# Weight decoding around the last attention group: bits moved from VectorE to ScalarE, a shorter PReLU, another order

## The chip, the cores and the metric

The kernel runs on one core of one Trainium2 chip. The metric is device time in microseconds. Three runs of the kernel before took 809.04, 806.07 and 810.14 us, a median of 809.04. Engines are named TensorE (PE: matmuls and transposes), ScalarE (ACT), VectorE (DVE), GpSimd (POOL) and SyncE (SP, which here issues nearly all loads).

## The reference

Three stages on 2304 tokens (4 batches of 576) of 512 features. Heads 0 to 3 attend to the last 32 positions, heads 4 to 7 to every 32nd:

```python
scores = np.where(masks, scale * q @ k.T, -1e9)      # 8 heads of 64
x = softmax(scores) @ v                              # -> (2304, 512)
h = x @ w_in                                         # 512 -> 2048
g = np.maximum(h, 0.0) + alpha * np.minimum(h, 0.0)  # PReLU, alpha per column
x = g @ w_out                                        # 2048 -> 512
logits = x @ w_gate; e = argmax(logits)              # 8 experts
y = np.maximum(x[e] @ w1[e], 0.0) @ w2[e]            # 512 -> 1024 -> 512
out = softmax(logits)[e] * sigmoid(x @ w_output_gate)[e] * y
```

`w_in` and `w_out` arrive as 64-bit floats, and the kernel turns them into 32-bit ones itself.

## The kernel before, in words

**Tiling.** The MLP's hidden dimension is cut into 16 parts of 128 (`NC1`), the tokens into 6 blocks of 384. One part of the weights is a tile of 128 x 1024 64-bit numbers, `w_in` and `w_out` side by side. Step n = 16 * block + part computes `mlp_in(n)` (12 matmuls of 384 columns into the bank `h`), PReLU (`mlp_act`), a split into high and low halves (`mlp_split`: `gh` by ScalarE, `gl` by VectorE) and `mlp_out(n)` (9 matmuls of 512 columns into three `acc` banks that gather over a block). Every product is computed in three matmuls, high by high, low by high, high by low, so that activations (`xh`, `xl`) and weights (`w`, 2048 wide, both halves) exist as pairs. `h` has two buffers: `mlp_in(n+2)` waits until `gl` of step n has read its bank.

**Decoding.** A part c goes through five operations before it can be used, each 128 x 1024: `decode_a` (ScalarE, L402, rescales the upper 32-bit word so that the exponent fits), `decode_b` (VectorE: L406 shifts left by three, L407 ORs in the top three bits of the lower word), `decode_s` (VectorE, L413, sets the sign), `decode_c` (ScalarE, L420, casts to the high half), `decode_d` (VectorE, L424, the low half). All 16 parts are decoded once, during the prologue and block 0.

**Order.** Every engine's instructions stand in the order in which the code is written; nothing is reordered. The prologue is a loop over 13 attention steps: step s computes the scores of group s, the exponentials and the norm of s - 1, the transposes of s - 2, the values of s - 3 with their store (ScalarE: `xh`) and rest (VectorE: `xl`, L372). Groups 0 to 9 cover what block 0 of the MLP needs; the last of them is group 9, whose rest is in step 12. Between these, decoding of part k starts in step 2 + 2k (`T0`) and advances by one operation per step, so parts 0 to 4 are begun there, and the first quarters of `mlp_in(0)` and `mlp_in(1)` are spread over steps 10 to 12 (`PRE`). Behind the prologue stand the last quarters of these two, their PReLU and split, 7 filler matmuls (`WAKE`), and the rest of the decoding of part 3. Then the loop over n: its iteration n issues `mlp_in(n+2)`, `mlp_act(n+2)`, parts of the decoding of n + 4, n + 5 and n + 6, `mlp_out(n)`, `mlp_split(n+2)`, and in the first 14 iterations of a block the pieces of one attention group for the next blocks. The bank `T` is shared by the transposes and the values of these groups: the transposes wait until the `xl` of the values before has been taken out.

**Loads** go out on SyncE in program order: `qk`, `v`, weight parts (`load_ws`). The router's weights are split once into `wg_hl`, in step 4 of the prologue.

Of the kernel before, what the change touches and what calls it, by code (L numbers as in the profile page):

```python
# [15 lines left out]
P = 128  # L16
# [8 lines left out]
E = 8  # L25
# [29 lines left out]

WHEN = ((0, 7), (1, 1), (1, 1), (1, 4), (1, 6))

NRV = range(FIRST)
FS = {2: 2}

PRE = {10: ((0, range(2)),), 11: ((0, range(2, 3)), (1, range(2))), 12: ((1, range(2, 3)),)}
QL = 96
RS = 7
NEG = -1.0e9
BIG = 12582912.0
SIGN = -(2**31)

C_ID = 0
C_I8 = C_ID + P
# [14 lines left out]
def attention_prelu_mlp_routed_experts_kernel(  # L84
# [19 lines left out]

    cst = base.tile([P, C_END], F32, name="cst")
    alpha_sb = base.tile([P, NC1], F32, name="alpha_sb")
    nalpha = base.tile([P, NC1], F32, name="nalpha")
    wg_sb = base.tile([P, KD, 2 * E], F32, name="wg_sb")
    cst16 = base.tile([P, W_END], BF16, name="cst16")
    wg_hl = base.tile([P, KD, 4 * E], F32R, name="wg_hl")  # L110
# [14 lines left out]
    with tc.manual_schedule():  # L125
# [47 lines left out]
        def load_v(n):  # L173
            b, pr, gs = visits[n]
            c = slice(2 * gs[0], 2 * gs[-1] + 2) if pr < 2 else slice(0, 5)
            t = v_t[n] = apool.tile([P, 6, 2, D], F32, tag="v", name="v", bufs=3)
            src = qkv[b, pr, :, 2 * S :].rearrange("p (i h d) -> p i h d", i=6, h=2)
            nc.sync.dma_start(t[:, c], src[:, c])
# [217 lines left out]
        def words(c):  # L396
            two = raw_t[c].rearrange("p (n two) -> p n two", two=2)
            return two[:, :, 0], two[:, :, 1]

        def decode_a(c):  # L400
            t = dec_t[c] = stage()[:, :1024]
            nc.scalar.activation(out=t, in_=words(c)[1].bitcast(F32), func=AF.Copy, scale=2.0**-112)  # L402

        def decode_b(c):
            t = dec_t[c].bitcast(I32)
            nc.vector.tensor_scalar(out=t, in0=t, scalar1=3, scalar2=None, op0=ALU.logical_shift_left)  # L406
            nc.vector.scalar_tensor_tensor(  # L407
                out=t, in0=words(c)[0], scalar=29, in1=t, op0=ALU.logical_shift_right, op1=ALU.bitwise_or
            )

        def decode_s(c):
            t = dec_t[c].bitcast(I32)
            nc.vector.scalar_tensor_tensor(  # L413
                out=t, in0=words(c)[1], scalar=SIGN, in1=t, op0=ALU.bitwise_and, op1=ALU.bitwise_or
            )
            raw_t.pop(c)

# [29 lines left out]
        def mlp_act(n):  # L447
            c = n % NC1
            ph = h_t.pop(n)
            v = ph[:, :BLK]  # L450
            a = xpool.tile([P, BLK], F32, tag="a", name="a", bufs=2)
            nc.scalar.activation(out=a, in_=v, func=AF.Relu)  # L452
            nc.scalar.activation(out=v, in_=v, func=AF.Relu, scale=-1.0)  # L453
            nc.vector.scalar_tensor_tensor(  # L454
                out=v, in0=v, scalar=nalpha[:, c : c + 1], in1=a, op0=ALU.mult, op1=ALU.add
            )
            h_t[n] = v

# [614 lines left out]

        load_qk(0)
        nc.vector.memset(zeros, 0.0)
        nc.scalar.activation(out=nalpha[:, 0:1], in_=zeros[:, 0:1], func=AF.Exp)
        warm(bank("acc0"), WARM)
        loads = iter(range(NC1))

# [11 lines left out]
        nc.sync.dma_start(alpha_sb, alpha)  # L1091
        nc.sync.dma_start(wg_sb, wg)
        load_qk(2)
        load_qk(3)
        load_v(2)
        load_ws(1)

        span = [0, FIRST + EXTRA]
        on = lambda g: span[0] <= g < span[1]
# [28 lines left out]

        steps_of = [(0, FIRST + LV), (FIRST + EXTRA, 23), (23, 31), (31, 39), (39, NG + LV)]
        NPRO = steps_of[0][1]  # L1130
        T0 = [2 + 2 * k for k in range(DEC + 1)]
        steps_done = {}

        def decode(k, n):
# [6 lines left out]
        for s in range(NPRO):  # L1141
            att_step(s, ("h", "h") if s % 2 else ("S", "X"), "acc0" if s % 2 else "T", "acc1" if s % 2 else "acc2")
            for n, ks in PRE.get(s, ()):
                mlp_in(n, ks)
            if s % 2 == 0:
                load_ws(1)
            if s == 4:
                nc.vector.tensor_scalar_mul(nalpha, alpha_sb, -1.0)
                nc.scalar.activation(out=wg_hl[:, :, : 2 * E], in_=wg_sb, func=AF.Copy)
                nc.vector.tensor_tensor(  # L1150
                    out=wg_hl[:, :, 2 * E :], in0=wg_sb, in1=wg_hl[:, :, : 2 * E].bitcast(F32), op=ALU.subtract
                )
                nc.vector.memset(acc_oh[:, 0, :], 0.0)
            for k in range(len(T0)):
                if 0 <= s - T0[k] and s < NPRO - 1:
                    decode(k, s - T0[k] + 1)

        span[:] = [FIRST + EXTRA if EXTRA < LV else 0, NG]
        for n in range(2):
            mlp_in(n, range(KD - 1, KD))  # L1160
            mlp_act(n)
            mlp_split(n)
        warm(bank("acc0"), WAKE)
        decode(DEC - 1, 5)
        decode(DEC, 3)
        decode(DEC + 1, 1)
        last = NBLK * NC1
        turn_at, logits_at = {}, {}
        for blk in range(NBLK - 1):
# [13 lines left out]
        for n in range(last):  # L1183
# [324 lines left out]
```

## Time and profile before

| | |
|---|---|
| median of three runs | 809.04 us (806.07 to 810.14) |
| profiled execution | 808.35 us, span 806.6 us |
| TensorE busy | 779.9 us, 97% of the span |
| VectorE busy | 469.7 us, 58% |
| ScalarE busy | 427.8 us, 53% |
| GpSimd busy | 90.9 us, 11% |
| mean granted clock of TensorE | 0.99 of full speed |

Busy shares are means over the whole span. The prologue lies in the first 45 us, block 0 of the MLP ends near 146 us, the blocks of the MLP end near 540 us, and the experts take the rest. A wait that the profile shows on an engine is idle time just before an instruction, with what ended it.

### The profile page before, as it was taken

What the parts mean: (1) busy time and instruction counts of PE and PEld (TensorE: products, weight loads), DVE (VectorE), ACT (ScalarE), POOL (GpSimd) and SP (SyncE); (2) the same over time, 40 slices, a digit from 0 to 9 for tenths busy, and PEclk for the clock granted to TensorE, in tenths of its full rate; (3) what the DMA queues carried; (4) which work ended last, traced back from release to release, by engine and by line L of the source; (5) the groups of instructions that cost most, each with busy time, mean ns of one, the idle gap of its engine ahead of it and who ended that gap; (6) DMA issues with size and microseconds to landing.
All of it is one profiled execution on the core that took longest, in us unless ns stands there. A gap on an engine that the chain in (4) does not pass through costs nothing.

```text
span 806.6 us, 13674 instructions
## 1 busy us (share of the span) xinstructions
PE 779.9 (97%) x5050; PEld 655.1 (81%) x5050; DVE 469.7 (58%) x1041; ACT 427.8 (53%) x1057; POOL 90.9 (11%) x91
## 2 busy tenths in 40 slices
PE   8798999999999999999999999999999999999996
PEld 4476777888888888888898888889889877978884
DVE  5989995346434553556233434668696557855432
ACT  6867785454544454645343333265544558665442
POOL 0001111011101011111000000100202121213201
PEclk9999999999999999999999999999999999999998
DMA  9818212012100131101000100543225578867510
GB/s 333 327 40 358 100 38 81 1 34 86 64 2 18 31 108 47 47 1 40 1 1 1 40 1 1 224 181 118 67 71 191 187 280 297 304 237 260 198 66 32
DMA packets 22620, 91.04 MB, mean 113 GB/s; under 512 B 3082, under 2 KB 7312, under 8 KB 15376
## 3 DMA queue, kind: packets, MB, share of 16 engines
q1 hardware_dynamic: 18816, 78.52, 26.5%
q0 software_dynamic: 3728, 11.55, 4.1%
q8 instruction: 42, 0.69, 0.3%
q14 instruction: 34, 0.28, 0.1%
HBM read 105.78 MB, written 9.97 MB: 144 GB/s over the span
## 4 chain that ended last, share of the span: by engine, by line
PE 77%; DVE 12%; issue 4%; ACT 3%; DMA 3%; SPq 0%; another core or an unknown queue 0%; POOL 0%; ACTq 0%; POOLq 0%; DVEq 0%
PE acc L1054 10%; PE acc L477 8%; PE h L444 7%; PE h L443 7%; PE h L445 7%; PE acc L479 7%; PE acc L478 7%; PE T L328 2%; PE sl_bank L234 2%; DMA raw<-in_wp_dram 2%; DVE stage L407 2%; PE T L313 2%; PE h L977 1%; DVE w L424 1%; PE h L978 1%
## 5 line engine op out<-in xcount | busy, mean ns | idle before, releaser
L900 DVE TENSOR_TENSOR wx<-raw,wx 128x1024 fp32r<-128x1024 f32 x96 | 112.1, 1220 | 41.5 <-ACT wx L899 38.2
L443 PE MATMUL h<-xh,w 128*128 128x384 f32 x384 | 129.7, 338 | 1.1 <-DVE gl L464 0.8
L444 PE MATMUL h<-xl,w 128*128 128x384 f32 x384 | 129.2, 337 | 0.7 <-DVE xl L372 0.7
L445 PE MATMUL h<-xh,w 128*128 128x384 f32 x384 | 129.0, 336 | 0.0
L454 DVE SCALAR_TENSOR_TENSOR h<-h,nalpha,a 128x384 f32<-128x384 f32 x96 | 59.9, 624 | 113.9 <-ACT h L453 113.9
L477 PE MATMUL acc<-w,gh 128*128 128x512 f32 x288 | 125.0, 434 | 0.0
L479 PE MATMUL acc<-w,gl 128*128 128x512 f32 x288 | 114.3, 397 | 0.0
L478 PE MATMUL acc<-w,gh 128*128 128x512 f32 x288 | 114.0, 396 | 0.0
L452 ACT ACTIVATE a<-h 128x384 f32<-128x384 f32 x96 | 47.2, 491 | 102.5 <-PE h L445 102.4
L899 ACT ACTIVATE wx<-raw 128x1024 fp32r<-128x1024 f32 x96 | 94.8, 1056 | 6.4 <-DMA raw<-in_wexp_dram 6.4
L1054 PE MATMUL acc<-wx,hh 128*128 128x512 f32 x304 | 96.9, 400 | 0.0
L443 PEld LDWEIGHTS h<-xh,w 128*128 128x128 f32 x384 | 72.3, 188 | 6.5 <-DVE gl L464 1.8
L444 PEld LDWEIGHTS h<-xl,w 128*128 128x128 f32 x384 | 72.2, 188 | 4.9 <-DVE xl L372 1.0
L297 POOL TENSOR_TENSOR p<-p,sm 96x512 f32<-96x512 f32 (+2 forms) x38 | 35.6, 936 | 345.3 <-DVE sm L296 239.6
L445 PEld LDWEIGHTS h<-xh,w 128*128 128x128 f32 x384 | 72.2, 188 | 0.0
L464 DVE TENSOR_TENSOR gl<-h,gh 128x384 fp32r<-128x384 f32 x96 | 53.3, 555 | 31.9 <-PE acc L479 17.2
L1054 PEld LDWEIGHTS acc<-wx,hh 128*128 128x128 f32 x304 | 56.4, 190 | 11.2
L479 PEld LDWEIGHTS acc<-w,gl 128*128 128x128 f32 x288 | 54.5, 189 | 13.2
L463 ACT ACTIVATE gh<-h 128x384 fp32r<-128x384 f32 x96 | 46.7, 486 | 34.3 <-DVE h L454 34.1
L477 PEld LDWEIGHTS acc<-w,gh 128*128 128x128 f32 x288 | 54.3, 189 | 10.6 <-issue 0.3
L1054 PE MATMUL acc<-wx,hl 128*128 128x512 f32 x152 | 60.1, 395 | 0.0
L478 PEld LDWEIGHTS acc<-w,gh 128*128 128x128 f32 x288 | 54.8, 190 | 5.5
(257 smaller groups left out, 1399.5 us busy)
## 6 DMA issues: line engine op xcount, KB each, us to landing
raw<-in_wexp_dram SPq DMA_DIRECT2D x64, 1024.0 KB
raw<-in_wp_dram SPq DMA_DIRECT2D x16, 1024.0 KB
qk<-in_qkv_dram SPq DMA_DIRECT2D x10, 576.0 KB
rows<-stage SPq DMA_DIRECT2D x15, 256.5 KB
v<-in_qkv_dram SPq DMA_DIRECT2D x8, 320.0 KB
qk<-in_qkv_dram SPq DMA_DIRECT2D x4, 384.0 KB
v<-in_qkv_dram SPq DMA_DIRECT2D x6, 256.0 KB
qk<-in_qkv_dram SPq DMA_DIRECT2D x4, 224.0 KB
```

Source lines behind the costliest of these rows:

```text
L443: mm(ph[:, :BLK], w_in(c, 0, k), xh[:, k, :], start=(k == 0), stop=False)
L444: mm(ph[:, :BLK], w_in(c, 0, k), xl[:, k, :], start=False, stop=False)
L445: mm(ph[:, :BLK], w_in(c, 1, k), xh[:, k, :], start=False, stop=(k == KD - 1))
L452: nc.scalar.activation(out=a, in_=v, func=AF.Relu)
L454: nc.vector.scalar_tensor_tensor(out=v, in0=v, scalar=nalpha[:, c : c + 1], in1=a, op0=ALU.mult, op1=ALU.add)
L464: nc.vector.tensor_tensor(out=gl, in0=v, in1=gh.bitcast(F32), op=ALU.subtract)
L477: mm(o, gh[:, t], w_out(c, 0), start=(c == 0), stop=False)
L478: mm(o, gh[:, t], w_out(c, 1), start=False, stop=False)
L479: mm(o, gl[:, t], w_out(c, 0), start=False, stop=(c == NC1 - 1))
L899: nc.scalar.activation(out=w[:, :1024], in_=raw, func=AF.Copy)
L900: nc.vector.tensor_tensor(out=w[:, 1024:], in0=raw, in1=w[:, :1024].bitcast(F32), op=ALU.subtract)
L1054: mm(po[i], h[:, h0 : h0 + P], wk[:, w0 : w0 + 512], start=st, stop=sp)
```

## The change

- *Six parts, three bits.* For the even parts from 4 on (`TAIL`: 4, 6, 8, 10, 12, 14) ScalarE writes the top three bits of the lower word into the low 16 bits of the upper word, in the raw tile, right behind `decode_a`; it reads and writes 16-bit integers that lie eight bytes apart. VectorE leaves out the OR of L407 there, and `decode_s` takes sign and tail in one mask (`SIGN + 7`).
- *PReLU.* ScalarE computes relu(-h) once into the SBUF tile `a`, and VectorE h + (1 - alpha) * a. The second ScalarE operation goes; `nalpha` becomes `calpha`.
- *Order.* A table (`DEC_AT`) says in which prologue step which part is taken how far. Part 2 is finished in step 12 behind the last group's rest; part 3 gets only shift and OR in the prologue, its sign, cast and low half stand behind the first PReLU; part 4 is begun behind them and finished in iteration 0 of the loop, ahead of part 5. The first three quarters of `mlp_in(1)` are split differently over step 12 and behind.
- *Loads.* The second weight part is loaded ahead of `v` 2 and `qk` 3.
- *Router.* `wg_hl` and a small memset move from prologue step 4 to iteration 13.

```diff
+TAIL = range(4, NC1, 2)
-PRE = {10: ((0, range(2)),), 11: ((0, range(2, 3)), (1, range(2))), 12: ((1, range(2, 3)),)}
+PRE = {10: ((0, range(2)),), 11: ((0, range(2, 3)),), 12: ((1, range(2)),)}
+DEC_AT = {
+    2: ((0, 1),),
+    3: ((0, 2),),
+    4: ((0, 3), (1, 1)),
+    5: ((0, 4), (1, 2)),
+    6: ((0, 5), (1, 3), (2, 1)),
+    7: ((1, 4), (2, 2)),
+    8: ((1, 5), (2, 3), (3, 1)),
+    10: ((2, 4), (3, 2)),
+    12: ((2, 5),),
+}
+SIGN_AND_TAIL = SIGN + 7
@@ decode_a
             nc.scalar.activation(out=t, in_=words(c)[1].bitcast(F32), func=AF.Copy, scale=2.0**-112)
+            if c in TAIL:
+                q = raw_t[c].bitcast(U16).rearrange("p (n four) -> p n four", four=4)
+                nc.scalar.activation(
+                    out=q[:, :, 2], in_=q[:, :, 1], func=AF.Copy, scale=2.0**-13, bias=2.0**-14 - 0.5
+                )
@@ decode_b
             nc.vector.tensor_scalar(out=t, in0=t, scalar1=3, scalar2=None, op0=ALU.logical_shift_left)
-            nc.vector.scalar_tensor_tensor(
-                out=t, in0=words(c)[0], scalar=29, in1=t, op0=ALU.logical_shift_right, op1=ALU.bitwise_or
-            )
+            if c not in TAIL:
+                nc.vector.scalar_tensor_tensor(
+                    out=t, in0=words(c)[0], scalar=29, in1=t, op0=ALU.logical_shift_right, op1=ALU.bitwise_or
+                )
@@ decode_s
-                out=t, in0=words(c)[1], scalar=SIGN, in1=t, op0=ALU.bitwise_and, op1=ALU.bitwise_or
+                scalar=SIGN_AND_TAIL if c in TAIL else SIGN,
...
@@ mlp_act
-            nc.scalar.activation(out=a, in_=v, func=AF.Relu)
-            nc.scalar.activation(out=v, in_=v, func=AF.Relu, scale=-1.0)
+            nc.scalar.activation(out=a, in_=v, func=AF.Relu, scale=-1.0)
             nc.vector.scalar_tensor_tensor(
-                out=v, in0=v, scalar=nalpha[:, c : c + 1], in1=a, op0=ALU.mult, op1=ALU.add
+                out=v, in0=a, scalar=calpha[:, c : c + 1], in1=v, op0=ALU.mult, op1=ALU.add
             )
@@ loads
         load_qk(2)
+        load_ws(1)
+        load_v(2)
         load_qk(3)
-        load_v(2)
-        load_ws(1)
@@ prologue loop
             if s == 4:
-                nc.vector.tensor_scalar_mul(nalpha, alpha_sb, -1.0)
-                nc.scalar.activation(out=wg_hl[:, :, : 2 * E], in_=wg_sb, func=AF.Copy)
...
+                nc.vector.tensor_scalar(
+                    out=calpha, in0=alpha_sb, scalar1=-1.0, scalar2=1.0, op0=ALU.mult, op1=ALU.add
+                )
-            for k in range(len(T0)):
-                if 0 <= s - T0[k] and s < NPRO - 1:
-                    decode(k, s - T0[k] + 1)
+            for k, n in DEC_AT.get(s, ()):
+                decode(k, n)
@@ behind the prologue
-        for n in range(2):
-            mlp_in(n, range(KD - 1, KD))
-            mlp_act(n)
-            mlp_split(n)
+        mlp_in(0, range(KD - 1, KD))
+        mlp_in(1, range(2, KD))
         warm(bank("acc0"), WAKE)
+        mlp_act(0)
+        mlp_split(0)
+        mlp_act(1)
+        decode(DEC - 1, 3)
+        mlp_split(1)
         decode(DEC - 1, 5)
-        decode(DEC, 3)
-        decode(DEC + 1, 1)
+        decode(DEC, 1)
@@ loop over n
+            if n == 0:
+                decode(DEC, 5)
             if n + DEC + 1 < NC1:
                 decode(n + DEC + 1, 3)
...
+            if n == NC1 - 3:
+                nc.scalar.activation(out=wg_hl[:, :, : 2 * E], in_=wg_sb, func=AF.Copy)
...
```

In the rows of order that follow, `raw_192`, `raw_279`, `raw_367` and `raw_364` are the raw tiles of parts 3, 4 and 5 (5 has another number after), `raw_454` and `raw_451` that of part 6, `acc_506`/`acc_499`, `acc_543`/`acc_536` and `acc_574`/`acc_556` the values of groups 7, 8 and 9; a stage tile without a raw one beside it is the part being shifted or subtracted. VectorE at the end of the prologue, before, from the rest of group 7 to the first PReLU:

```order
L372 TENSOR_TENSOR xl<-acc_506,xh 128x2x12x7
L372 TENSOR_TENSOR xl<-acc_506,xh 128x2x6x7
L424 TENSOR_TENSOR w<-stage,w 128x1024
L413 SCALAR_TENSOR_TENSOR stage<-raw_192,stage 128x1024
L372 TENSOR_TENSOR xl<-acc_543,xh 128x2x12x7
L372 TENSOR_TENSOR xl<-acc_543,xh 128x2x6x7
L406 TENSOR_SCALAR stage<-stage 128x1024
L407 SCALAR_TENSOR_TENSOR stage<-raw_279,stage 128x1024
L372 TENSOR_TENSOR xl<-acc_574,xh 128x12x4
L372 TENSOR_TENSOR xl<-acc_574,xh 128x6x4
L454 SCALAR_TENSOR_TENSOR h<-h,nalpha,a 128x384
```

The same place of VectorE after the change:

```order
L388 TENSOR_TENSOR xl<-acc_499,xh 128x2x12x7
L388 TENSOR_TENSOR xl<-acc_499,xh 128x2x6x7
L427 TENSOR_SCALAR stage<-stage 128x1024
L429 SCALAR_TENSOR_TENSOR stage<-raw_192,stage 128x1024
L388 TENSOR_TENSOR xl<-acc_536,xh 128x2x12x7
L388 TENSOR_TENSOR xl<-acc_536,xh 128x2x6x7
L388 TENSOR_TENSOR xl<-acc_556,xh 128x12x4
L388 TENSOR_TENSOR xl<-acc_556,xh 128x6x4
L451 TENSOR_TENSOR w<-stage,w 128x1024
L481 SCALAR_TENSOR_TENSOR h<-a,calpha,h 128x384
L491 TENSOR_TENSOR gl<-h,gh 128x384
```

Part 3's shift and OR (which stood ahead of group 9's norm) now stand behind group 7's rest; part 2's low half moved behind group 9's rest, and part 3's sign and part 4's shift and OR have left this place. VectorE from the second split of the start to the split of iteration 0, before:

```order
L464 TENSOR_TENSOR gl<-h,gh 128x384
L424 TENSOR_TENSOR w<-stage,w 128x1024
L413 SCALAR_TENSOR_TENSOR stage<-raw_279,stage 128x1024
L454 SCALAR_TENSOR_TENSOR h<-h,nalpha,a 128x384
L406 TENSOR_SCALAR stage<-stage 128x1024
L407 SCALAR_TENSOR_TENSOR stage<-raw_367,stage 128x1024
L413 SCALAR_TENSOR_TENSOR stage<-raw_367,stage 128x1024
L424 TENSOR_TENSOR w<-stage,w 128x1024
L464 TENSOR_TENSOR gl<-h,gh 128x384
```

VectorE at the same place after the change:

```order
L491 TENSOR_TENSOR gl<-h,gh 128x384
L451 TENSOR_TENSOR w<-stage,w 128x1024
L481 SCALAR_TENSOR_TENSOR h<-a,calpha,h 128x384
L427 TENSOR_SCALAR stage<-stage 128x1024
L435 SCALAR_TENSOR_TENSOR stage<-raw_279,stage 128x1024
L451 TENSOR_TENSOR w<-stage,w 128x1024
L427 TENSOR_SCALAR stage<-stage 128x1024
L429 SCALAR_TENSOR_TENSOR stage<-raw_364,stage 128x1024
L435 SCALAR_TENSOR_TENSOR stage<-raw_364,stage 128x1024
L491 TENSOR_TENSOR gl<-h,gh 128x384
```

Part 3's sign now stands just ahead of these rows, between the second PReLU and its split; part 4's shift, sign and low half stand ahead of part 5 and so of the `gl` of iteration 0, and no OR is there for part 4. ScalarE from the first PReLU of the start to the split of iteration 0, before:

```order
L452 ACTIVATE a<-h 128x384
L453 ACTIVATE h<-h 128x384
L463 ACTIVATE gh<-h 128x384
L452 ACTIVATE a<-h 128x384
L453 ACTIVATE h<-h 128x384
L463 ACTIVATE gh<-h 128x384
L402 ACTIVATE stage<-raw_367 128x1024
L452 ACTIVATE a<-h 128x384
L453 ACTIVATE h<-h 128x384
L420 ACTIVATE w<-stage 128x1024
L402 ACTIVATE stage<-raw_454 128x1024
L463 ACTIVATE gh<-h 128x384
```

ScalarE at the same place after the change:

```order
L490 ACTIVATE gh<-h 128x384
L480 ACTIVATE a<-h 128x384
L490 ACTIVATE gh<-h 128x384
L447 ACTIVATE w<-stage 128x1024
L418 ACTIVATE stage<-raw_279 128x1024
L421 ACTIVATE raw_279<-raw_279 128x1024
L480 ACTIVATE a<-h 128x384
L447 ACTIVATE w<-stage 128x1024
L418 ACTIVATE stage<-raw_364 128x1024
L418 ACTIVATE stage<-raw_451 128x1024
L421 ACTIVATE raw_451<-raw_451 128x1024
L490 ACTIVATE gh<-h 128x384
```

One activation per PReLU is gone. Between the second `gh` and the PReLU of iteration 0 stand the cast of part 3 (L447), `decode_a` of part 4 (L418) and the new pass (L421, raw to raw); parts 5 and 6 follow behind the cast of part 4, with the pass of part 6 ahead of the last `gh`.

## Rows read from the trace of the kernel before

**Rows 1.** First part of the page: busy us, share of the span, instructions per engine.
```profile
PE 779.9 (97%) x5050; PEld 655.1 (81%) x5050; DVE 469.7 (58%) x1041; ACT 427.8 (53%) x1057; POOL 90.9 (11%) x91
```

**Rows 2.** Stretches: from:to us, length, busy us per engine, clock, DMA share, GB/s.
```profile
20.00:40.00 20.00, 15.38 (x113) 9.21 (x114) 19.07 (x47) 17.98 (x67) 0.00 (x0) 0.91 0.84 334
...
60.00:80.00 20.00, 16.78 (x97) 13.14 (x96) 19.66 (x33) 15.86 (x45) 3.09 (x3) 0.94 0.90 359
...
80.00:130.00 50.00, 48.62 (x323) 38.58 (x323) 45.67 (x88) 38.02 (x119) 7.05 (x8) 0.99 0.24 80
...
100.00:120.00 20.00, 19.44 (x130) 15.56 (x129) 19.69 (x36) 17.00 (x55) 2.48 (x3) 1.00 0.13 39
...
140.00:540.00 400.00, 398.89 (x2395) 342.91 (x2393) 189.90 (x536) 182.26 (x541) 28.41 (x30) 1.00 0.13 47
```

**Rows 3.** TensorE's waits, 45 to 140 us: waiter, releaser, us in total, times, longest.
```profile
PE T L313 <- DVE xl L372: 3.6, 4, 2.2
```

**Rows 4.** Timeline of TensorE: start, duration, line, operands, shapes, idle before and releaser.
```profile
37.66 0.65 PE L313 MATMUL T<-cst,p 126*126 126x126 f32 x4 [1.55 <-DVE p L297]
...
44.19 0.44 PE L443 MATMUL h<-xh,w 128*128 128x384 f32 x1 [0.25 <-ACT xh L367]
...
45.37 0.44 PE L444 MATMUL h<-xl,w 128*128 128x384 f32 x1 [0.74 <-DVE xl L372]
...
58.27 0.37 PE L443 MATMUL h<-xh,w 128*128 128x384 f32 x1
...
77.06 0.69 PE L313 MATMUL T<-cst,p 126*126 126x126 f32 x4 [2.21 <-DVE xl L372]
...
79.26 0.63 PE L478 MATMUL acc<-w,gh 128*128 128x512 f32 x1
...
86.83 0.34 PE L443 MATMUL h<-xh,w 128*128 128x384 f32 x1
...
131.25 0.39 PE L479 MATMUL acc<-w,gl 128*128 128x512 f32 x1
...
131.48 0.34 PE L443 MATMUL h<-xh,w 128*128 128x384 f32 x1
...
137.66 0.34 PE L443 MATMUL h<-xh,w 128*128 128x384 f32 x1
```

**Rows 5.** Timeline of VectorE, 63 to 77 us: two `gl` in a row.
```profile
63.49 0.55 DVE L464 TENSOR_TENSOR gl<-h,gh 128x384 fp32r<-128x384 f32 x1
...
69.66 0.55 DVE L464 TENSOR_TENSOR gl<-h,gh 128x384 fp32r<-128x384 f32 x1
```

**Rows 6.** Timeline of VectorE, 18 to 46 us, the prologue.
```profile
18.99 0.21 DVE L1150 TENSOR_TENSOR wg_hl<-wg_sb,wg_hl 128x64 fp32r<-128x64 f32 x1
...
21.42 0.17 DVE L295 TENSOR_SCALAR sm<-sm 126x4 f32<-126x4 f32 x1 [0.41 <-ACT p L281]
...
40.59 1.21 DVE L424 TENSOR_TENSOR w<-stage,w 128x1024 fp32r<-128x1024 f32 x1
...
41.73 1.21 DVE L413 SCALAR_TENSOR_TENSOR stage<-raw,stage 128x1024 int32<-128x1024 int32 x1
...
43.97 1.23 DVE L407 SCALAR_TENSOR_TENSOR stage<-raw,stage 128x1024 int32<-128x1024 int32 x1
...
45.11 0.29 DVE L372 TENSOR_TENSOR xl<-acc,xh 128x48 fp32r<-128x48 f32 x2
```

**Rows 7.** Timeline of ScalarE, 18 to 47 us.
```profile
18.61 1.16 ACT L402 ACTIVATE stage<-raw 128x1024 f32<-128x1024 f32 x1 [1.50 <-DMA raw<-in_wp_dram]
...
46.02 0.49 ACT L452 ACTIVATE a<-h 128x384 f32<-128x384 f32 x1 [1.81 <-PE h L445]
...
46.41 0.49 ACT L453 ACTIVATE h<-h 128x384 f32<-128x384 f32 x1
```

**Rows 8.** All instructions of one line: count, duration min/median/max in ns, first and last start.
```profile
L402 ACT ACTIVATE stage<-raw x16: 1122/1148/1167, 11.1 to 111.7; 128x1024 f32<-128x1024 f32 x16
...
L407 DVE SCALAR_TENSOR_TENSOR stage<-raw,stage x16: 1224/1226/1226, 15.8 to 118.8; 128x1024 int32<-128x1024 int32 x16
```

More of the change, by code (lines that the diff above doesn't have):

```diff
@@ L9 @@
 F32R = mybir.dt.float32r
+U16 = mybir.dt.uint16
 BF16 = mybir.dt.bfloat16
@@ L106, in attention_prelu_mlp_routed_experts_kernel @@
     alpha_sb = base.tile([P, NC1], F32, name="alpha_sb")
-    nalpha = base.tile([P, NC1], F32, name="nalpha")
+    calpha = base.tile([P, NC1], F32, name="calpha")
     wg_sb = base.tile([P, KD, 2 * E], F32, name="wg_sb")
@@ L413, in decode_s @@
             nc.vector.scalar_tensor_tensor(
-                out=t, in0=words(c)[1], scalar=SIGN, in1=t, op0=ALU.bitwise_and, op1=ALU.bitwise_or
+                out=t,
+                in0=words(c)[1],
+                scalar=SIGN_AND_TAIL if c in TAIL else SIGN,
+                in1=t,
+                op0=ALU.bitwise_and,
+                op1=ALU.bitwise_or,
             )
@@ L1075, in attention_prelu_mlp_routed_experts_kernel @@
         nc.vector.memset(zeros, 0.0)
-        nc.scalar.activation(out=nalpha[:, 0:1], in_=zeros[:, 0:1], func=AF.Exp)
+        nc.scalar.activation(out=calpha[:, 0:1], in_=zeros[:, 0:1], func=AF.Exp)
         warm(bank("acc0"), WARM)
@@ L1130, in attention_prelu_mlp_routed_experts_kernel @@
         NPRO = steps_of[0][1]
-        T0 = [2 + 2 * k for k in range(DEC + 1)]
         steps_done = {}
@@ L1147, in attention_prelu_mlp_routed_experts_kernel @@
             if s == 4:
-                nc.vector.tensor_scalar_mul(nalpha, alpha_sb, -1.0)
-                nc.scalar.activation(out=wg_hl[:, :, : 2 * E], in_=wg_sb, func=AF.Copy)
-                nc.vector.tensor_tensor(
-                    out=wg_hl[:, :, 2 * E :], in0=wg_sb, in1=wg_hl[:, :, : 2 * E].bitcast(F32), op=ALU.subtract
-                )
-                nc.vector.memset(acc_oh[:, 0, :], 0.0)
-            for k in range(len(T0)):
-                if 0 <= s - T0[k] and s < NPRO - 1:
-                    decode(k, s - T0[k] + 1)
+                nc.vector.tensor_scalar(
+                    out=calpha, in0=alpha_sb, scalar1=-1.0, scalar2=1.0, op0=ALU.mult, op1=ALU.add
+                )
+            for k, n in DEC_AT.get(s, ()):
+                decode(k, n)
         span[:] = [FIRST + EXTRA if EXTRA < LV else 0, NG]
-        for n in range(2):
-            mlp_in(n, range(KD - 1, KD))
-            mlp_act(n)
-            mlp_split(n)
+        mlp_in(0, range(KD - 1, KD))
+        mlp_in(1, range(2, KD))
         warm(bank("acc0"), WAKE)
+        mlp_act(0)
[3 more added lines that the diff above has]
+        mlp_split(1)
         decode(DEC - 1, 5)
-        decode(DEC, 3)
-        decode(DEC + 1, 1)
+        decode(DEC, 1)
         last = NBLK * NC1
@@ L1235, in attention_prelu_mlp_routed_experts_kernel @@
                 mlp_split(n + 2)
+            if n == NC1 - 3:
+                nc.scalar.activation(out=wg_hl[:, :, : 2 * E], in_=wg_sb, func=AF.Copy)
+                nc.vector.tensor_tensor(
+                    out=wg_hl[:, :, 2 * E :], in0=wg_sb, in1=wg_hl[:, :, : 2 * E].bitcast(F32), op=ALU.subtract
+                )
+                nc.vector.memset(acc_oh[:, 0, :], 0.0)
             if c == NC1 - 1 and blk == 3:
```

## The prediction

> **What bounds the kernel now.** I began with the page's first part: TensorE is busy for 779.9 of 806.6 us [rows 1]. So nearly everything hangs on TensorE, and a change elsewhere can win only where TensorE waits or runs slowly. The stretches tell where that is [rows 2]. From 140 to 540 us it is idle for 1.1 us of 400 while VectorE is under half busy: nothing off TensorE moves the time there. From 20 to 40 us it is idle for 4.6 us, from 60 to 80 us for 3.2 us at a mean clock of 0.94, from 80 to 130 us for 1.4 us. In 20 to 40 and 60 to 80 us VectorE is busy for 19.07 and 19.66 of 20 us, from 100 to 120 us for 19.69. It decodes the weights there, and this is what the change touches.
>
> TensorE's waits between 45 and 140 us name the releaser [rows 3]: VectorE's `xl`, attention's remainder, 3.6 us. In order of time: at 77.06 TensorE waits 2.21 us for the T bank, which this `xl` frees, and the matmuls behind it show 0.63 us where one of their kind shows 0.39 at 131.25: the lower of the two clock levels, 1.2 GHz [rows 4]. Where TensorE alone decides, a step with attention takes 137.66 - 131.48 = 6.18 us; from 86.83 to 131.48 seven steps take 6.38 each, 1.4 us over in all [rows 4]. VectorE's step is as long: `gl` follows `gl` by 69.66 - 63.49 = 6.17 us [rows 5]. Two engines with the same period: relief of VectorE is worth something only until TensorE's 6.18 is reached.
>
> The last wait before the loop is the other place: TensorE sits until 45.37 for the last group's `xl` [rows 4], which VectorE does at 45.11 behind decoding of parts 2, 3 and 4 [rows 6].
>
> **The change part by part.** *End of the prologue.* Ahead of the last `xl` VectorE runs L424 (1.21), L413 (1.21) and a shift with L407 (1.23) between 40 and 45.11 us [rows 6]; part 3's shift and OR stand before these. Afterwards only part 3's shift and OR remain ahead of it, where VectorE waits for TensorE and ScalarE anyway. What is late next is TensorE's own queue: before, it ran from the transposes at 37.66 to the first missing `xh` (0.25 us before 44.19) without a wait, 6.28 us [rows 4]; the three matmuls that end this stretch now stand behind the first product's last three, so the length stays. Its start comes 0.65 us sooner: the subtraction of `wg_hl` (0.21) leaves VectorE's queue, and VectorE's wait of 0.41 us at 21.42 goes [rows 6], because ScalarE no longer waits 1.50 us at 18.61 for the second weight part [rows 7], whose load goes out ahead of one `qk` and one `v` load. These two land later, at worst when that part landed before, near 18.6, and attention step 7 needs them first, three steps on: cost nothing; with that cover gone it would be the 1.5 us back. So the first PReLU activation starts at 37.0 + 6.3 = 43.3 instead of 46.02 [rows 7]: 2.7 us earlier.
>
> *Filling the loop.* That work was moved, not removed. Behind the first activation VectorE now has part 3's sign and subtraction and part 4's shift, sign and subtraction, all before part 5's and before `gl` of step 2, for which TensorE's third product (58.27 before [rows 4]) waits. ScalarE stands in it too: the cast of part 3, L402 of part 4 and its new pass come before the activation of step 2, so VectorE waits about 1.4 us there, and 1.0 us for the cast of part 4. With the durations of rows 6 and 8: activation of step 2 at 43.3 + 7.0 = 50.3; VectorE's PReLU at 50.8, shift and sign to 53.2, subtraction 54.2 to 55.3, part 5 to 58.3, `gl` to 58.8. The third product starts at 58.9, 0.6 us later than before. TensorE (fillers to 46.1, then two products and two outputs of 2.1 each, 12 matmuls 0.174 and 9 matmuls 0.234 us apart, and scores of 1.0) is through at 55.5 and idle for 3.4 us; it may lose its clock, which is hidden, since its next scores wait for exponentials till about 62.6. The 2.7 us are spent.
>
> *One OR less in six parts.* L407 costs 1.226 us [rows 8]; parts 4, 6, 8, 10, 12 and 14 lose it, 7.4 us of VectorE. Part 4's is in the sum above; from step 1 on every second step of VectorE is 1.2 us shorter than 6.17, the mean about 5.6, under TensorE's 6.18. Carried on with the same durations, `gl` of step 3 starts at 62.9, 0.6 us earlier than at 63.49, and two steps on another 1.2; the wait of 2.21 us at 77.06 goes, and with it the slow stretch (six matmuls of 512 columns at 0.2 us more, two of 384 at 0.15: 1.5). So of 2.2 + 1.5 = 3.7 the 0.5 that is still owed goes off: the product at 86.83 [rows 4] starts at 83.6, 3.2 us gained. From there TensorE can gain its remaining 1.4 us.
>
> *The new ScalarE pass.* No row shows 2-byte elements eight bytes apart. The nearest is L402, which reads the same tile at the same step: 1.148 us [rows 8], and I take that. Below, it could halve with the bytes (0.57); above, double if two-byte writes run apart (2.3). ScalarE's own bound on the step: 17.00 us in 20 us [rows 2] is 5.45 per step of 6.41, less 0.39 for the PReLU activation (start to start, 46.02 to 46.41 [rows 7]), 5.06; with the pass 6.2, about TensorE's 6.18. So in a tail step ScalarE has no room, and the exponentials behind it come late; I charge 0.1 us for four such steps, 0.4. The Trainium skill speaks against the move: "ScalarE: Activation LUTs", section "Rules for kernel authors", gives additions and multiplications to VectorE, as up to about three times as fast per element there in bf16. The trace disagrees for this pair, 1.226 against 1.148 [rows 8].
>
> *PReLU.* L453 goes (0.49 us, 96 times [rows 7]); VectorE's operation keeps one operand in PSUM, and I take its time as unchanged (between 0.55, the row of `gl` [rows 5], and 0.7). Off block 0 the shorter chain is slack: it is worth between 0 and TensorE's 1.1 idle us of 140 to 540 [rows 2], and I take 0. The `wg_hl` pair moves to step 13 of block 0, where the decoding is over and its reader is a block away: nothing.
>
> Sum: 3.2 + 1.4 - 0.4 = 4.2. The profiled execution took 808.35 us (span 806.6), so 804.15 in its terms; it lies 0.7 under the median of the runs, 809.04, so I forecast 804.8.
>
> **Rivals.** *Nothing is spent on filling.* If the third product starts 2.7 us earlier too, the gain is that plus the idle 3.2 and 1.4 us of 60 to 130 [rows 2] plus 1.5 of slow clock, 8.8: 800.2. For it: less ScalarE work per step, and the pass may be short. Against it: VectorE's order, with 5 us of decoding ahead of that product.
>
> *The fill costs more.* If the 3.4 us of idle TensorE bring the low clock and the slow product pushes scores and exponentials, the loop starts some 2 us further behind, and the relief of the ORs meets TensorE's 6.18 before it is made good: 3.2 - 2.0 = 1.2 is left: 807.8. For it: the stall at 77.06 was followed by slow matmuls [rows 4]. Against it: the slack before the exponentials.
>
> *ScalarE takes VectorE's place (slower).* At 2.3 us per pass, ScalarE's tail step is 5.06 + 2.3 = 7.4, 1.2 over TensorE's 6.18. Six such steps cost 7.1, since ScalarE works in order and has the exponentials and the cast of the next weight part behind the pass: 804.8 + 7.1 = 811.9. It decides from 1.12 us per pass on, and eats the whole gain at 1.8. For it: such an access is in no row. Against it: L402 on the same bytes. By the skill's factor of three on 1.226 the pass would be an estimated 3.7 us and the time about 820.
>
> **How the numbers follow.** Forecast 0.58 (its own range 801.5 to 807.5), no fill cost 0.17, costlier fill 0.15, ScalarE 0.10. What a measurement of this kernel can tell from no change is 0.5%, 4 us, so the line is at 805.0. The forecast lies just on the fast side: 0.34 of its 0.58 there; with 0.17 faster is 0.51. Same: 0.24 + 0.15 + 0.03 of the ScalarE case, 0.42. Slower: 0.07. The range 800.0 to 809.5 leaves out half of the second case and most of the ScalarE one.
>
> **What would show it.** In the new profile: the first PReLU activation near 43.3; the third product of the loop near 58.9 with some 3 us of idle TensorE ahead; no wait of TensorE for `xl` over 1 us; VectorE with gaps of about 1 us in every second step between 75 and 120; the product that started at 86.83 near 83.6, the one at 137.66 near 133.5; the new pass at 1.1 to 1.2 us; from 140 us on the same spacing as before. Wrong it is if the pass takes 1.8 us or more, if the third product starts before 57 or after 60.5, or if TensorE waits for ScalarE's exponentials more than 1 us in all between 85 and 130.

## The result, and the profile after

The changed kernel takes 817.21 us (median of 5 runs, 815.63 to 818.81) against 809.04 for the kernel before on the same chip, a ratio of 1.0103 [1.008 to 1.0127]: 8.2 us slower. I had forecast 804.8 and faster. Its profiled execution took 818.81 us (span 816.6).

The first part of the page of the changed kernel gives each engine's busy us, share of the span and instructions:

```profile
PE 785.2 (96%) x5050; PEld 661.0 (81%) x5050; DVE 463.4 (57%) x1035; ACT 405.2 (50%) x967; POOL 91.8 (11%) x91
```

Beside [rows 1]: TensorE has as many matmuls and is busy 5.3 us longer, so part of the loss is matmuls at the lower clock; the other part is waiting. The stretches of the changed kernel (start:end, length, busy us and instructions of PE, PEld, DVE, ACT, POOL, then granted clock, DMA share and GB/s) say where:

```profile
40.00:60.00 20.00, 15.32 (x86) 12.09 (x84) 12.98 (x19) 12.82 (x17) 0.00 (x0) 1.00 0.27 89
60.00:80.00 20.00, 17.85 (x96) 15.04 (x97) 17.77 (x32) 18.00 (x46) 3.09 (x3) 0.83 0.47 193
80.00:130.00 50.00, 45.41 (x291) 36.64 (x290) 41.91 (x82) 41.45 (x106) 5.59 (x7) 0.97 0.31 109
140.00:540.00 400.00, 399.19 (x2409) 343.07 (x2404) 187.62 (x536) 151.26 (x462) 29.00 (x31) 1.00 0.13 43
```

From 80 to 130 us TensorE is idle for 4.6 us, where [rows 2] have 1.4; from 60 to 80 us its mean clock is 0.83 against 0.94. From 140 to 540 us the stretch is again full. VectorE, busy for 19.66 of 20 us from 60 to 80 us before, has room now (17.77), and ScalarE rose there from 15.86 to 18.00, from 80 to 130 us from 38.02 to 41.45. TensorE's waits of the changed kernel, up to 150 us (who waits <- for whom: us in all, times, longest):

```profile
PE h L470 <- DVE gl L491: 6.0, 1, 6.0
PE sl_bank L244 <- ACT p L297: 3.7, 4, 1.5
PE sl_bank L244 <- DVE gl L491: 1.2, 1, 1.2
```

The `xl` that led [rows 3] is gone. In its place stand one wait of 6.0 us for `gl` and several for ScalarE's exponentials (`p`, L297). The same waits in order of time, with the first product of the loop's next block at the end (start, us, engine, line, operation, out<-in, [idle before <-releaser]; TensorE of the changed kernel):

```profile
61.35 0.69 PE L470 MATMUL h<-xh,w 128*128 128x384 f32 x1 [6.03 <-DVE gl L491]
61.83 0.52 PE L471 MATMUL h<-xl,w 128*128 128x384 f32 x1
...
86.10 0.27 PE L244 MATMUL sl_bank<-cst 96*96 96x256 bf16 x1 [1.47 <-ACT p L297]
...
90.37 0.63 PE L504 MATMUL acc<-w,gh 128*128 128x512 f32 x1
...
101.61 0.27 PE L244 MATMUL sl_bank<-cst 126*126 126x252 bf16 x1 [1.48 <-ACT p L297]
...
115.45 0.27 PE L244 MATMUL sl_bank<-cst 96*96 96x256 bf16 x1 [1.16 <-DVE gl L491]
...
143.70 0.34 PE L470 MATMUL h<-xh,w 128*128 128x384 f32 x1
```

The third product starts at 61.35 instead of 58.27 [rows 4], after a stall, and its matmuls take 0.52 us where 0.34 is the normal one: 1.2 GHz, until 67.3 (granted clock 0.51 from 61.0 to 67.3). Behind the wait at 86.10 the 512-column matmuls take 0.63 where 0.39 is normal, the same lower clock; behind the waits at 101.61 and 115.45 they do not. The product that stood at 137.66 [rows 4] stands at 143.70, so 6.0 us are lost by the end of block 0. The last PReLU of the loop begins at 541.8 (before 536.3), so 5.5 of them are left there.

What ScalarE does ahead of that `gl` (same columns, ScalarE of the changed kernel):

```profile
43.30 0.49 ACT L480 ACTIVATE a<-h 128x384 f32<-128x384 f32 x1 [1.46 <-PE h L472]
...
48.21 1.12 ACT L418 ACTIVATE stage<-raw 128x1024 f32<-128x1024 f32 x1
49.37 2.52 ACT L421 ACTIVATE raw<-raw 128x1024 uint16<-128x1024 uint16 x1
51.63 0.58 ACT L480 ACTIVATE a<-h 128x384 f32<-128x384 f32 x1
54.75 1.06 ACT L447 ACTIVATE w<-stage 128x1024 fp32r<-128x1024 f32 x1 [2.54 <-DVE stage L435]
55.72 2.14 ACT L418 ACTIVATE stage<-raw 128x1024 f32<-128x1024 f32 x2
57.89 2.50 ACT L421 ACTIVATE raw<-raw 128x1024 uint16<-128x1024 uint16 x1
60.13 0.57 ACT L490 ACTIVATE gh<-h 128x384 fp32r<-128x384 f32 x1
```

The first activation is at 43.30, as forecast. The new pass, L421, takes 2.5 us, not 1.148. It runs twice, for part 4 and part 6, ahead of `gh` at 60.13, which `gl` needs. All six, in the view of that line (min/median/max ns):

```profile
L421 ACT ACTIVATE raw<-raw x6: 2497/2570/2612, 49.4 to 111.9; 128x1024 uint16<-128x1024 uint16 x6
```

VectorE's PReLU is what I took it for (L481, median 0.621 us; before, L454, 0.626).

My theory from here: **the price of the pass makes the loss**. Rivals: **the order** (the last group's chain ahead of the decoding leaves a hole in front of the third product, whatever the pass costs), and **the PReLU form**.

### The profile page after: what moved, and what is told of

It reads as the page before. It is cut to its first block, busy times and chain, and to the rows that moved or that the text cites. A ratio compares the mean times of both kernels' runs of the same rounds, so it can differ in the third digit from the quotient of the medians.

```text
span 816.6 us, 13575 instructions
## 1 busy us (share of the span) xinstructions
PE 785.2 (96%) x5050; PEld 661.0 (81%) x5050; DVE 463.4 (57%) x1035; ACT 405.2 (50%) x967; POOL 91.8 (11%) x91
## 4 chain that ended last, share of the span: by engine, by line
PE 81%; DVE 9%; ACT 5%; issue 3%; DMA 2%; POOL 0%; ACTq 0%; POOLq 0%; DVEq 0%
PE acc L1081 10%; PE acc L504 9%; PE h L470 8%; PE h L472 8%; PE h L471 8%; PE acc L506 7%; PE acc L505 7%; PE sl_bank L250 3%; PE T L344 2%; PE T L329 2%; PE h L1004 2%; ACT raw L421 2%; PE h L1005 2%; PE h L1006 2%; DVE wx L927 1%
## 5 line engine op out<-in xcount | busy, mean ns | idle before, releaser
L481 DVE SCALAR_TENSOR_TENSOR h<-a,calpha,h 128x384 f32<-128x384 f32 x96 | 59.5, 620 | 87.1 <-ACT a L480 84.2
```

The source lines that it names most:

```text
L481: nc.vector.scalar_tensor_tensor(out=v, in0=a, scalar=calpha[:, c : c + 1], in1=v, op0=ALU.mult, op1=ALU.add)
```

## The experiments

All ratios below are against the kernel before, run on the same chip as the experiment.

**The pass taken out.** The changed kernel with VectorE's OR in all parts:

```
-TAIL = range(4, NC1, 2)
+TAIL = ()
```

> The changed kernel without the new ScalarE pass (all 16 parts get their OR on VectorE again); order, loads and PReLU stay changed. Pass theory: the pass, 2.57 us in the trace of after, is what made it slower; without it the activation of step 2 comes about 2.6 us earlier, the 6.03 us stall of TensorE shrinks to 3 us or less, no wait of 1.5 us for exponentials between 85 and 116 is left, and the time is 805 to 811, within 0.4% of the kernel before. Order theory: the postponed decoding makes the stall whatever ScalarE does; the stall stays at 5 us or more and the time at 814 or more.

Measured: 808.21 us against 808.05, 1.0003 [0.9979 to 1.0027]. The whole loss goes with the pass. TensorE of this run:

```profile
59.91 0.69 PE L470 MATMUL h<-xh,w 128*128 128x384 f32 x1 [4.19 <-DVE gl L491]
...
78.78 0.62 PE L329 MATMUL T<-cst,p 126*126 126x126 f32 x4 [1.66 <-DVE xl L388]
...
137.87 0.34 PE L470 MATMUL h<-xh,w 128*128 128x384 f32 x1
```

The time is what the pass theory expected. The hole in front of the third product is not: 4.19 us, between the 3 us or less of the pass theory and the 5 us or more of the order theory, so about two thirds of it come without the pass. The wait for `xl` is back, since VectorE has all its ORs again. Order and PReLU together are no measurable gain, and no loss of this size either.

**The pass alone,** on the kernel before: the ScalarE pass, the OR left out for parts 4, 6, ..., 14, and the wider mask.

```
+            if c in TAIL:
+                q = raw_t[c].bitcast(U16).rearrange("p (n four) -> p n four", four=4)
+                nc.scalar.activation(out=q[:, :, 2], in_=q[:, :, 1], func=AF.Copy, scale=..., bias=...)
...
```

> The kernel before with only the pass (six parts; OR left out there): order, loads and PReLU as before. Pass theory: ScalarE becomes the bound in the tail steps, and two passes fall into the prologue and the start; slower than before, 812 to 818. Order theory: VectorE is relieved of 7.4 us without any postponed work, so this is faster than before, 801 to 806.

Measured: 811.58 us against 808.05, 1.0044 [1.0022 to 1.0066]: the direction as expected, just under the expected stretch. Its line and its waits:

```profile
L407 ACT ACTIVATE raw<-raw 128x1024 uint16<-128x1024 uint16 x6 | 15.3, 2558 | 0.2
```

```profile
60.80 0.27 PE L230 MATMUL sl_bank<-cst 126*126 126x252 bf16 x1 [1.12 <-ACT p L283]
...
68.08 0.27 PE L230 MATMUL sl_bank<-cst 126*126 126x252 bf16 x1 [1.29 <-ACT p L283]
...
83.61 0.27 PE L230 MATMUL sl_bank<-cst 96*96 96x256 bf16 x1 [1.28 <-DVE gl L472]
...
97.56 0.27 PE L230 MATMUL sl_bank<-cst 126*126 126x252 bf16 x1 [1.52 <-ACT p L283]
...
111.52 0.27 PE L230 MATMUL sl_bank<-cst 96*96 96x256 bf16 x1 [1.27 <-DVE gl L472]
```

In the old order there is no hole in front of the third product, which starts at 57.33; what is left is a wait of 1.1 to 1.5 us behind each of the five passes from part 6 on. So the pass costs 0.44% in the old order, and in the new one 1.0103 / 1.0003, about 1.0%: the two parts of the change make each other worse. The traces say the same of block 0: the product of 137.66 starts at 140.13 here, 2.5 us later than before; in the new order the pass moves it from 137.87 to 143.70, by 5.8.

**PReLU alone,** on the kernel before:

```
-            nc.scalar.activation(out=a, in_=v, func=AF.Relu)
-            nc.scalar.activation(out=v, in_=v, func=AF.Relu, scale=-1.0)
+            nc.scalar.activation(out=a, in_=v, func=AF.Relu, scale=-1.0)
...
```

> The kernel before with only the shorter PReLU. Pass and order theory alike: VectorE stays full in block 0 and TensorE elsewhere, so the time is that of before within 0.3%, 807 to 810. If the shorter PReLU itself were to blame for part of the loss, it would be 811 or more; if it shortens a chain that matters, 805 or less.

Measured: 806.84 against 808.05, 0.9987 [0.9966 to 1.0008], just under the expected stretch. No loss comes from here. In its trace the product of 137.66 [rows 4] starts at 135.19; the interval doesn't tell whether anything of that stays. About 1.5 us of it is TensorE's clock and not a shorter chain. The wait of 2.21 us for `xl` is here as before [rows 4], but the 512-column matmuls behind it run at the full clock (0.39 us, before 0.63):

```profile
76.10 0.62 PE L313 MATMUL T<-cst,p 126*126 126x126 f32 x4 [2.21 <-DVE xl L372]
...
77.72 0.39 PE L478 MATMUL acc<-w,gl 128*128 128x512 f32 x1
```

From this wait's end to the product that stood at 86.83 it is 8.2 us here (76.10 to 84.30) and 9.8 before (77.06 to 86.83).

**The order alone,** with the loads and the router's weights, but neither pass nor new PReLU (the experiment without the pass, with the PReLU edit above turned back).

> The kernel before with only the new order (decoding table, loads, router weights later): no pass, old PReLU. Pass theory: the prologue ends 2.7 us earlier and the postponed decoding takes that back, 806 to 811. Order theory: 814 or more.

Measured: 810.35 against 808.05, 1.0026 [1.0004 to 1.0048]. The wait in front of the third product is 4.86 us (it starts at 60.95), the wait for `xl` of 2.21 us stands at 79.83, and the product of 137.66 at 138.92. Behind that wait for `xl` the matmuls run at the full clock too. The order by itself costs about a quarter of a per cent, at most half a per cent by its interval; as the cause of the 1% it falls.

**What makes the pass dear.** Extra copies on a weight tile that is no longer needed, one form for each of parts 5 to 15, added to the kernel before (its time of 813.53 us, one run, is that of the extra work). Shortened here: `q` is the tile as 16-bit numbers in groups of four (eight bytes), `w2` as 32-bit numbers in pairs, `flat` as 16-bit numbers in a row.

```
+            if c == 7:   act(flat[:, :512], q[:, 512:, 1])     # 2-byte read 8 bytes apart, dense write
+            if c == 8:   act(w2[:, :, 1], w2[:, :, 0])         # 4 bytes, 8 bytes apart
+            if c == 9:   act(w2[:, :, 1], q[:, :, 1])          # 2-byte read, 4-byte write
+            if c == 10:  act(q[:, :, 2], w2[:, :, 0])          # 4-byte read, 2-byte write
...
```

> The kernel before with one extra pass per part behind its sign, on the raw tile that nobody reads any more, for its duration alone: on ScalarE with scale and bias as in the change (part 5), without (6), 16-bit read at eight bytes and contiguous write (7, 512 columns), 32-bit word to 32-bit word at eight bytes (8), 16-bit read and 32-bit write (9), 32-bit read and 16-bit write (10), 16-bit contiguous (11), 16-bit at four bytes (12), contiguous read and 16-bit write at eight bytes (15, 512 columns); on VectorE a 16-bit shift (13); on GpSimd a 16-bit multiply-add (14). If the 16-bit write between other bytes is what costs, forms 5, 6, 10, 12 and 15 take about twice the 1.15 us (0.6 for 512 columns) of the others; if the 16-bit read does, 5, 6, 7, 9; if integers as such do, all of them; if it is scale and bias, 5 alone.

ScalarE of this run, the pass as it is first, then without scale and bias, then parts 7 to 10, 11 (2 bytes, dense on both sides), 12 (2 bytes, 4 bytes apart) and 15 (dense read, 2-byte write 8 bytes apart, 512 elements):

```profile
57.99 2.57 ACT L425 ACTIVATE raw<-raw 128x1024 uint16<-128x1024 uint16 x1 [0.36 <-DVE stage L414]
...
65.09 2.50 ACT L425 ACTIVATE raw<-raw 128x1024 uint16<-128x1024 uint16 x1
...
72.17 0.67 ACT L425 ACTIVATE raw<-raw 128x512 uint16<-128x512 uint16 x1
...
78.72 1.16 ACT L425 ACTIVATE raw<-raw 128x1024 int32<-128x1024 int32 x1
...
84.80 1.16 ACT L425 ACTIVATE raw<-raw 128x1024 int32<-128x1024 uint16 x1
...
91.44 2.56 ACT L425 ACTIVATE raw<-raw 128x1024 uint16<-128x1024 int32 x1
...
98.94 1.09 ACT L425 ACTIVATE raw<-raw 128x1024 uint16<-128x1024 uint16 x1
...
105.46 1.40 ACT L425 ACTIVATE raw<-raw 128x1024 uint16<-128x1024 uint16 x1
...
127.86 1.35 ACT L425 ACTIVATE raw<-raw 128x512 uint16<-128x512 uint16 x1
```

It is the write (one instance of each form). With a 4-byte write eight bytes apart the copy takes 1.16 us, whether it reads 2 or 4 bytes; with a 2-byte write there it takes 2.56, whatever it reads; 2-byte writes four bytes apart take 1.40, dense ones 1.09. Reading 2 bytes eight apart costs no more than reading 4 bytes there (1.16 both). Scale and bias cost nothing that shows (2.57 with, 2.50 without). I had expected the step of four bytes among the dear forms; at 1.40 it is not.

**The pass at the price that I took.** The changed kernel with the pass on 416 of the 1024 columns; the last three bits of the other columns of those six parts are left out.

```
-                    out=q[:, :, 2], in_=q[:, :, 1], ...
+                    out=q[:, :416, 2], in_=q[:, :416, 1], ...
```

> The changed kernel with the pass cut to 416 of 1024 columns (the last three bits of the other columns are left wrong), about 1.15 us each, the price that the prediction took. If that price was the only wrong term, the ratio to before is 0.993 to 0.997 and the stall before the third product 3 to 4 us. If the start was mis-sized as well, as the run without the pass suggests (its stall was 4.2 us), the ratio is 0.996 to 1.002. If the number of passes or their order rather than their length makes the loss, it stays at 1.006 or more.

Measured: 806.62 against 808.48, 0.9982 [0.9964 to 1.0]. Its pass and its TensorE:

```profile
L421 ACT ACTIVATE raw<-raw 128x416 uint16<-128x416 uint16 x6 | 6.9, 1158 | 0.2
```

```profile
59.49 0.44 PE L470 MATMUL h<-xh,w 128*128 128x384 f32 x1 [4.05 <-DVE gl L491]
...
134.06 0.34 PE L470 MATMUL h<-xh,w 128*128 128x384 f32 x1
```

At 1.158 us a pass, block 0 goes nearly as the prediction said: the product of 137.66 [rows 4] starts at 134.06 (forecast 133.5), and no wait for exponentials over 0.43 us is left in the loop. The ratio lies in the range that I had set for "the start was mis-sized as well", and the wait of 4.05 us is just over the 3 to 4 us of the price alone. From 134.06 to 143.70, 9.6 us, is what the pass's price costs in block 0.

**No pass in the start.** The changed kernel with the pass from part 8 on:

```
-TAIL = range(4, NC1, 2)
+TAIL = range(8, NC1, 2)
```

> The changed kernel with the pass for parts 8, 10, 12 and 14 only; parts 4 and 6 get their OR back. The two passes that stood in the start are gone: the stall before the third product is about 4.2 us as without any pass, while the waits of TensorE for exponentials or gl behind the later passes stay at 1.2 to 1.5 us each, four of them. Ratio 1.002 to 1.006, between the run without a pass and the changed kernel; if the early passes make no difference, 1.008 or more.

Measured: 814.88 against 808.48, 1.0074 [1.0051 to 1.0098], above what I expected. The third product starts at 59.89, as without a pass, but waits of 0.85, 1.41, 1.49 and 1.15 us behind the four remaining passes are there. In the traces the two early passes are about half of what the pass costs in block 0: the product of 137.66 stands at 137.87 without a pass, at 140.58 with the four late ones, at 143.70 with all six. By the medians (1.0003, 1.0074, 1.0103) the late ones weigh more. In this trace the rest of the loss lies behind block 0: from 540 us on it loses 4.7 us against the kernel before (see "What stays open"). Four late passes cost 2.7 us of block 0 here, six cost 2.5 in the old order. So what makes the new order dearer in block 0 is the two early passes. Why the medians put less on them is not settled.

**The same idea with 4-byte writes.** The changed kernel, but the pass turns the whole lower word into its top three bits, and VectorE shifts and ORs in one instruction:

```
+                nc.scalar.activation(out=lo, in_=lo.bitcast(U32), func=AF.Copy, scale=2.0**-29, bias=2.0**-20 - 0.5)
...
+                nc.vector.scalar_tensor_tensor(out=t, in0=t, scalar=3, in1=words(c)[0],
+                    op0=ALU.logical_shift_left, op1=ALU.bitwise_or)
...
```

> The changed kernel with another pass in the same six places: ScalarE reads the lower 32-bit word and writes its top three bits back as a whole 32-bit word, and VectorE shifts and ORs them in with one operation (1.22 us) instead of the shift (0.68) and the OR (1.23). If narrow writes are what costs, the pass takes 1.1 to 1.2 us instead of 2.57, no wait of TensorE over 1 us is left between 85 and 120, the stall before the third product is 4 to 5 us, and the ratio to before is 0.997 to 1.002. If a second pass of any form at this place does the harm, 1.006 or more.

Measured: 807.9 against 808.25, 0.9986 [0.9968 to 1.0003]; the pass:

```profile
L422 ACT ACTIVATE raw<-raw 128x1024 int32<-128x1024 uint32 x6 | 6.9, 1154 | 0.0
```

Same job, 1.154 us, and the loss is gone, with nothing left out. The wait ahead of the third product is 4.47 us, and no wait of TensorE over 1 us is left between 85 and 120, as expected.

**The old order with the 4-byte pass and the new PReLU** (passes on parts 6, 8, 10, 12, 14):

> The kernel before with the shorter PReLU and the 32-bit pass for parts 6, 8, 10, 12 and 14, decoding order and loads as before. VectorE is relieved of 0.69 us in every second step and nothing is postponed. If the order's fill is what eats the relief, this is faster than the shorter PReLU alone (0.9987) and than the changed kernel with the 32-bit pass: third product near 57.5, the wait at the T bank 1 us or less, ratio 0.994 to 0.998. If ScalarE has no room for 1.15 us, 0.999 or more.

Measured: 805.93 against 808.25, 0.9971 [0.9951 to 0.9992]. The third product starts at 57.60, no wait for `xl` at the T bank is left, one of 1.35 us for exponentials stands at 66.86, and the product of 137.66 is at 132.47, 5.2 us early.

**The same with the changed order of the loads and the router's weights later:**

```
+        load_ws(1)
+        load_v(2)
...
+            if n == NC1 - 3:
+                nc.scalar.activation(out=wg_hl[:, :, : 2 * E], in_=wg_sb, func=AF.Copy)
```

> As the kernel above, with the changed kernel's loads and the late router weights besides. The prologue's VectorE work begins 0.6 us earlier; where VectorE carries that through, the third product comes 0.6 us earlier and the ratio is 0.0005 to 0.001 lower, which these runs can hardly tell; 0.993 to 0.998.

Measured: 803.52 us (6 runs, 801.56 to 805.64) against 808.25, **0.9933 [0.9911 to 0.9954]**: faster than both kernels. Its profiled execution is the longest of the six, so its trace says little of the median: in it the product of 137.66 stands at 135.93, later than the 132.47 of the kernel above, behind a wait of 2.21 us for exponentials at 67.51 and the lower clock after it (0.57 from 67 to 75 us). So where this kernel's gain arises is not shown.

## Why the prediction was wrong

**The step that failed is the price of the pass.** I wrote: "The nearest is L402, which reads the same tile at the same step: 1.148 us [rows 8], and I take that", with 2.3 as the upper bound. It takes 2.57 us, outside my bounds. L402 reads the tile at that step but writes densely into another tile [rows 8]; the pass writes two bytes of every eight. I took the row that matched in what it reads, and what it writes sets the time. The upper bound named the cause ("if two-byte writes run apart") but went by a doubling. The price is most of the miss, not all of it: the forecast was a ratio of 0.9948 (804.8 of 809.04), the short pass gives 0.9982 [0.9964 to 1.0], the full one 1.0103.

**What followed from that price, in the prediction's own terms.** The rival "ScalarE takes VectorE's place" is what happened: place, mechanism and sign, priced at 811.9 for 2.3 us a pass. At 2.57, its tail step is 5.06 + 2.57 = 7.63 us, 1.45 over TensorE's 6.18, and the waits behind the later passes are 1.47, 1.48 and 1.16. It got a chance of 0.10. At 2.57 us the rival's own sum would be six times 1.45, 8.7 us, so 813.5; 817.21 was measured. Beside it stood a rule of the Trainium skill ("ScalarE: Activation LUTs", section "Rules for kernel authors"), that VectorE is the engine for additions and multiplications. I had set it aside on the 4-byte pair of [rows 8]. For 4-byte writes the runs still show nearly equal times (1.154 on ScalarE, 1.226 on VectorE); for the 2-byte write of this pass VectorE does a shift in 1.337 us where ScalarE takes 2.57, so here the rule pointed the right way, by a factor of 1.9 and for a shift, which is neither addition nor multiplication.

Two things were missing in the rival: the passes of parts 4 *and* 6 stand in the start, ahead of `gl` of step 2; and a wait can bring the lower clock. From the run with the short pass to the changed kernel the lag of TensorE's products grows like this (starts of the same products, each from its trace):

```
product          short pass   2.57 us pass   lag
third               59.49        61.35       1.9
two steps on        72.22        76.03       3.8
was at 86.83        84.59        91.42       6.8
two steps on        97.44       105.69       8.3
two steps on       109.55       119.19       9.6
was at 137.66      134.06       143.70       9.6
```

1.9 is the start. Of the next 1.9, 0.9 come from the longer stretch at 1.2 GHz (from 61.35 to 67.3; with the short pass from 60.65 to about 64.4), 1.1 from waits of TensorE for the exponentials and `gl` near 72. The 3.0 after it is the wait of 1.47 with slow matmuls behind it (0.63 us at 90.37). Then 1.4 comes twice, with no slow matmuls: that is what the pass is longer (2.57 less 1.16).

**What held.** The first activation at 43.30 (forecast 43.3). The fill: with the pass at the price I took, the activation of step 2 is at 50.41 (50.3) and the third product at 59.49 (58.9), with 4.05 us of idle TensorE where I had said 3.4. The relief of VectorE: in the runs with the ORs taken out at most 0.26 us of the wait for `xl` at the T bank is left, and 0.56 us with the word pass in the new order. PReLU: no gain beyond its interval. From 140 to 540 us: unchanged.

**What held only in part.** With the short pass block 0 gains 3.6 of the 4.2 us forecast in its trace, but the medians show 1.9. One term of the forecast's sum belonged to the execution that was profiled: the 1.5 us of slow matmuls behind the wait at 77.06. The same wait of 2.21 us is in the traces of "PReLU alone" and "the order alone", without them. How many executions of the kernel before have them, the runs do not show. The low clock in the fill was hidden only in part: with the short pass TensorE waits 0.23 us for exponentials (63.17) behind the slow product, but from there to the first output matmul it takes 1.22 us, a step later 0.84. The order was worth less than I gave it: the 2.7 us won ahead of the loop go in the fill, as said, and the old order with the 4-byte pass and the loads (0.9933) beats the new order with that pass (0.9986) by more than their intervals.

**What stays open.** 6.0 us are lost in block 0, 8.2 in the medians, 10.5 between the two profiled executions. In the profiled execution the rest comes behind 540 us, where the changed kernel shows three stretches at 0.83 of the clock:

```profile
560.00:570.00 10.00, 10.00 (x75) 10.00 (x75) 7.38 (x26) 3.16 (x7) 1.51 (x3) 0.83 0.59 226
...
610.00:620.00 10.00, 10.00 (x54) 8.41 (x55) 6.25 (x17) 5.70 (x7) 1.01 (x1) 0.83 0.66 226
...
690.00:700.00 10.00, 8.57 (x57) 8.37 (x58) 8.28 (x11) 6.88 (x11) 3.89 (x3) 0.83 0.95 352
```

Wherever such stretches occur in the traces, they stand at the same three places of the program, 23 to 27, 66 to 71 and 148 to 153 us after the last PReLU begins (a short one in the last 7 us left out). The kernel before has the second of them, the changed kernel all three, the experiments none to three. The time from the last PReLU to the end goes with their number: 268.9 to 270.7 us with none or one (before 270.3), 271.7 to 273.2 with two, 273.1 to 275.0 with three (274.8 here). No part of the change works there. The three traces with the pass at its full length in the loop (the changed kernel, "the pass alone", "no pass in the start") have all three; the other nine have two at most, the run with the extra copies, three of them of 2.5 us and more, none. With one trace of each kernel that may be chance; what sets their number was not tried.

## What to carry to other kernels

Price a new instruction by a row that matches it in what it writes, in width and step, not only in what it reads; where no row does, measure the one instruction before the design rests on it. When work goes from one engine to another in a loop in which both run near the period of the bounding engine, add it to the receiver's step first: here 5.06 us left 1.12 for the pass, and at 2.57 the 1.45 us above that came back as a wait of 1.2 to 1.5 us behind each of the last three passes. Ahead of a loop, an engine that works in order makes everything moved onto it part of the fill, so test such a move in both orders. And a slow stretch that is counted into a gain should be looked for in a second execution: the one behind the wait at 77.06 was not in the other two traces with that wait.

## What the runs showed of the hardware

- ScalarE copies of 128x1024 with 2-byte writes eight bytes apart: 2.50 to 2.61 us; from 512 elements (1.35) to 1024 (2.56) is 1.21 us, 2.4 ns per element. 4-byte writes at the same step: 1.13 to 1.18; 2-byte writes four bytes apart: 1.40; dense: 1.09.
- The same 2-byte step on the other engines, in the run with the extra copies (view of the line, min/median/max ns): a shift on VectorE and a multiply-add on GpSimd.

```profile
L443 DVE TENSOR_SCALAR raw<-raw x1: 1337/1337/1337, 112.4 to 112.4; 128x1024 uint16<-128x1024 uint16 x1
...
L445 POOL TENSOR_SCALAR raw<-raw x1: 3253/3253/3253, 120.5 to 120.5; 128x1024 uint16<-128x1024 uint16 x1
```

- The lower clock came behind each wait of 4 us and more ahead of the third product, but not at the same place: behind 6.03 us (61.35, the changed kernel) and 4.19 us (59.91, without the pass) from the first matmul on, behind 4.86 us (60.95, the order alone) from the second or third, behind 4.47 us (59.70, the word pass) from the third, behind 4.05 us (59.49, the short pass) only from the seventh, at 60.65 (0.33 to 0.35 us for the five before it, 0.52 behind).
- Behind shorter waits it came in some executions and not in others: behind 2.21 us for `xl` in the kernel before (granted clock 0.58 from 77 to 80 us), not in the PReLU alone (1.00 from 77 to 80) nor in the order alone (1.00 from 80 to 83); in the changed kernel behind 1.47 us (86.10; 0.50 from 88 to 90), not behind 1.48 (101.61; 1.00 from 101 to 108).
